# A Fourier stage on two column halves of the array, with one evacuation per PSUM bank, late inputs prepared later, and a load split over two queues

## The chip, the cores and the metric

The kernel runs on one core of a Trainium2 chip. The metric is the device time of one execution in microseconds (us). All runs told here are of the fast state (the granted TensorE clock is 0.97 of full speed on average in all of them). "TensorE" is called PE in the profile and its weight loads PEld; VectorE is DVE, ScalarE is ACT, GpSimd is POOL, SyncE is SP. PSUM is the memory that takes TensorE's results, in banks; an evacuation is the copy that moves a bank's content out of it. A unit is the work on four channels: two calls of the transform stage.

## The reference

A long convolution (by FFT along the sequence), then a maxout FFN:

```python
def _attn_ref(x, v, pos_emb, w1, w2):              # B=4, S=12544, D=128
    h_filt = (np.maximum(pos_emb @ w1, 0.0) @ w2) * window
    u = x * v
    L = 2 * S
    Uf = np.fft.rfft(u, n=L, axis=1)
    Hf = np.fft.rfft(h_filt, n=L, axis=0)
    y = np.fft.irfft(Uf * Hf[None, :, :], n=L, axis=1)[:, :S, :]
    return (x * y).astype(np.float32)

def _moe_ref(x, w1, w2, w3, w_out):                # 50176 tokens, 768 hidden
    h = np.maximum(np.maximum(x @ w1, x @ w2), x @ w3)
    return h @ w_out
```

Everything is float32. The kernel writes 12544 as 98 x 128. Its first transform stage is a 98-point transform over one index, as a matmul with the constant `f1` (98 x 196: 98 columns of real parts, 98 of imaginary parts).

## The kernel before

`first` is the stage that changes. One call handles two channels: two matmuls of 98 rows, 128 weight columns (`lhs[i]`: two interleaved halves r of 64 points) and 196 moving columns. The result lies in one PSUM bank with r on the partitions and (channel, real/imaginary c, frequency k) on the columns. `spec` wants c on the partitions, so four copies of 64 partitions move it, two on each engine.

```python
    def first(ps, lhs, at):
        for i in range(2):
            nc.tensor.matmul(ps[:, i * 2 * NB:(i + 1) * 2 * NB], lhs[i], f1[:],
                             start=(i == 0), stop=True, skip_group_check=True)
        for r in range(2):
            for c in range(2):
                src = ps[64 * r:64 * r + 64, 0:4 * NB].rearrange(
                    "p (s c k) -> p c k s", s=2, c=2)[:, c]
                dst = spec[64 * c:64 * c + 64, :, r, at:at + 2]
                if r == 0:
                    nc.scalar.copy(dst, src)
                else:
                    nc.vector.tensor_copy(dst, src)
```

It is called 64 times for the filter (stretch A), 64 times for batch 0 (32 units of two calls, stretch B), and 64 times for each of batches 1 to 3, there between the FFN's matmuls of the batch before:

```python
    def u_first(u):                      # one unit: two calls
        t = uts.pop(u)
        for i in range(2):
            ps = state["turn"][1].tile([P, 512], FP32, tag="cv", name="ps1")
            first(ps, [...], 4 * u + 2 * i)
    # ... stretch B (the first NPRE = 20 units are transposed beforehand)
    for u in range(NU):
        u_first(u)
        v = u + NPRE
        if v < NU:
            u_mul(v)                     # VectorE: x * v of a late unit
        if u and v - 1 < NU:
            u_turn(v - 1)                # TensorE: its four transpositions
            if v + 2 < NU:
                u_load(0, v + 2)
    # ... beside the FFN, one unit in 1.9 slots of the FFN
            at(s, u_turn, u)
            at(s + 1, u_first, u)
```

For each of 49 groups of frequencies, `g_load` brings weights and the filter's spectrum `ht` (two halves of 64 partitions) through SyncE's queue.

## Time and profile before

| stretch | us | what sets it |
|---|---|---|
| A: filter's first stage, 86.33 to 137.73 | 51.4 | VectorE's copies |
| A to B: second stage of the filter, preparations of batch 0 | 93.6 | loads |
| B: batch 0's first stage, 231.28 to 305.74 | 74.5 | late loads, then copies |
| batch 0's groups alone, to the first FFN work | 247.1 | serial work of VectorE and ScalarE |
| long part, from 552.82 | 2293.0 | TensorE |
| whole execution | 2847.86 (median) | |

A and B run to the first record of the second stage (L144); the long part starts at the first record of L477. A row of the windows has the length of the stretch, then each engine's busy time with the number of its records, the granted clock, the DMA engines' busy share and GB/s. A float32 matmul leaves two records.

### The profile page before, as it was taken

The numbers are of one execution on the slowest core, as the hardware profiler recorded it, in microseconds if no ns is written. First come the engines' busy times: TensorE is split into PE (matmuls) and PEld (weight loads), VectorE is DVE, ScalarE is ACT, GpSimd is POOL, SyncE is SP. The second block draws the span as 40 slices with busy tenths as digits, with TensorE's granted clock in tenths as the row PEclk, the third lists the DMA queues.
The fourth block names the chain that finished last, engine by engine and source line by source line (L and its number), as shares of the span: only waits on it lengthen the run. The fifth ranks groups of instructions, "written<-read, shape, count | busy, mean of one in ns | idle before, by whom it ended". The sixth has DMA issues, their size and how long they took to land.

```text
span 2845.9 us, 38675 instructions
## 1 busy us (share of the span) xinstructions
PE 2650.9 (93%) x13277; PEld 1926.9 (68%) x13277; DVE 1539.4 (54%) x3265; ACT 1196.9 (42%) x2571; POOL 26.9 (1%) x53
## 2 busy tenths in 40 slices
PE   6967665599999999999999999999999999999999
PEld 6866655477777676677777676777767766666665
DVE  3866777555466666355566665454666663222222
ACT  2635544344444444344444443444444442222222
POOL 0021000000000000000000000000000000000000
PEclk9988777799999999999999999999999999999999
DMA  3198599644577776444678774445687872222221
GB/s 78 38 354 230 156 266 280 193 105 100 139 212 220 212 220 185 110 98 108 173 215 222 221 217 129 105 113 142 183 224 216 223 197 68 57 57 57 56 56 34
DMA packets 455348, 446.12 MB, mean 157 GB/s; under 512 B 292746, under 2 KB 344432, under 8 KB 454960
## 3 DMA queue, kind: packets, MB, share of 16 engines
q1 hardware_dynamic: 329392, 353.27, 46.9%
q10 hardware_dynamic: 121840, 77.52, 9.3%
q0 software_dynamic: 3920, 12.85, 1.2%
q8 instruction: 106, 1.74, 0.3%
q14 instruction: 90, 0.74, 0.1%
HBM read 353.61 MB, written 89.92 MB: 156 GB/s over the span
## 4 chain that ended last, share of the span: by engine, by line
PE 75%; ACT 3%; DMA 2%; ACTq 0%; DVE 0%; issue 0%; SPq 0%; DVEq 0%
PE pa L489 17%; PE pb L492 17%; PE ops L500 17%; PE yps L477 8%; PE ps L128 4%; PE ps L420 4%; PE ps L144 3%; PE ops L499 3%; PE pst L356 1%; DMA ht<-hd 1%; ACT xs L395 1%; ACT xs L394 1%; ACT zs L424 1%; DMA zt<-zd 1%; ACT hid L490 1%; ACT eo L156 0%
## 5 line engine op out<-in xcount | busy, mean ns | idle before, releaser
L493 DVE TENSOR_TENSOR hid<-hid,pb 128x392 f32<-128x392 f32 x768 | 431.3, 562 | 582.4 <-PE pb L492 468.5
L489 PE MATMUL pa<-gt,w_sb 128*128 128x392 f32 x1536 | 638.2, 497 | 11.8 <-ACT hid L490 11.2
L490 ACT ACTIVATE hid<-pa 128x392 f32<-128x392 f32 x768 | 382.5, 498 | 615.1 <-PE pa L489 541.2
L492 PE MATMUL pb<-gt,w_sb 128*128 128x392 f32 x1536 | 632.0, 493 | 1.2 <-ACT hid L490 1.2
L500 PE MATMUL ops<-hid,wo_sb 128*128 128x392 f32 x1536 | 630.9, 492 | 0.1
L492 PEld LDWEIGHTS pb<-gt,w_sb 128*128 128x128 f32 x1536 | 289.8, 190 | 218.6 <-DVE hid L493 25.5
L500 PEld LDWEIGHTS ops<-hid,wo_sb 128*128 128x128 f32 x1536 | 291.7, 190 | 214.2 <-DVE hid L493 0.7
L489 PEld LDWEIGHTS pa<-gt,w_sb 128*128 128x128 f32 x1536 | 258.2, 191 | 114.5 <-ACT hid L490 45.3
L420 PE MATMUL ps<-ab,wt 128*128 128x128 f32 x1568 | 231.8, 295 | 96.1 <-DVE ab L411 96.1
L138 DVE COPY spec<-ps 64x196 f32<-64x196 f32 x640 | 235.6, 368 | 149.1 <-ACT spec L136 139.8
L420 PEld LDWEIGHTS ps<-ab,wt 128*128 128x128 f32 x1568 | 217.6, 205 | 139.6 <-issue 68.8
L144 PE MATMUL ps<-spec,wt 128*128 128x128 f32 x1960 | 287.8, 298 | 9.8 <-DVE spec L138 9.8
L144 PEld LDWEIGHTS ps<-spec,wt 128*128 128x128 f32 x1960 | 273.9, 215 | 24.6 <-issue 10.3
L136 ACT COPY spec<-ps 64x196 f32<-64x196 f32 x640 | 214.8, 336 | 166.0 <-PE ps L128 154.0
L477 PEld LDWEIGHTS yps<-f,zt 98*128 98x128 f32 x2048 | 250.5, 193 | 43.2 <-DMA zt<-zd 7.9
L400 DVE TENSOR_TENSOR xt<-xt,ht 128x512 f32<-128x512 f32 x196 | 135.5, 691 | 241.7 <-ACT xs L395 234.4
L477 PE MATMUL yps<-f,zt 98*128 98x98 f32 x2048 | 248.1, 274 | 7.6 <-DMA zt<-zd 7.6
L424 ACT COPY zs<-ps 128x512 f32<-128x512 f32 x196 | 114.9, 586 | 259.0 <-PE ps L420 246.2
L394 ACT ACTIVATE xs<-xt 64x512 f32<-64x512 f32 x196 | 123.0, 628 | 171.3 <-DVE xt L151 138.5
L128 PEld LDWEIGHTS ps<-f,uT 98*128 98x128 f32 x1024 | 175.9, 193 | 25.1
L481 DVE TENSOR_TENSOR gt<-yps,xT 128x392 f32<-128x392 f32 x128 | 72.5, 566 | 221.7 <-PE yps L477 210.6
L128 PE MATMUL ps<-f,uT 98*128 98x196 f32 x1024 | 192.4, 334 | 0.0
(58 smaller groups left out, 1710.2 us busy)
## 6 DMA issues: line engine op xcount, KB each, us to landing
wt<-wt_const SPq DMA_DIRECT2D x220, 512.0 KB
ht<-hd SPq DMA_DIRECT2D x392, 256.0 KB
zd<-zs ACTq DMA_DIRECT2D x196, 256.0 KB
zt<-zd SPq DMA_DIRECT2D x128, 392.0 KB
ut<-in_xr_dram SPq DMA_DIRECT2D x128, 196.0 KB
ut<-in_vr_dram SPq DMA_DIRECT2D x128, 196.0 KB
xT<-in_x_dram SPq DMA_DIRECT2D x512, 49.0 KB
out_dram<-ot ACTq DMA_DIRECT2D x128, 196.0 KB
```

The lines of the kernel that those rows point to most:

```text
L128: nc.tensor.matmul(ps[:, i * 2 * NB:(i + 1) * 2 * NB], lhs[i], f1[:], start=(i == 0), stop=True, skip_group_check=True)
L136: nc.scalar.copy(dst, src)
L138: nc.vector.tensor_copy(dst, src)
L144: nc.tensor.matmul(ps[:, (2 * k + r) * D:(2 * k + r + 1) * D], w[:, k, r, :], spec[:, 2 * g + k, r, :], start=(k == 0 and r == 0), stop=Tr ...
L394: nc.scalar.mul(xs[0:64], xt[64:128], -1.0)
L420: nc.tensor.matmul(ps[:, (2 * k + q) * D:(2 * k + q + 1) * D], w[:, 1, k, q, :], ab[:, k, q, :], start=(k == 0 and q == 0), stop=True, ski ...
L477: nc.tensor.matmul(ps[:, s * NB:(s + 1) * NB], zt[:, c, s * D:(s + 1) * D], f4[:, c, :], start=(s == 0 and c == 0), stop=(c == 1), skip_gr ...
L489: nc.tensor.matmul(pa[:, 0:N], w_sb[1][:, f * P:(f + 1) * P], rhs, start=True, stop=True)
L490: nc.scalar.activation(h[:], pa[:, 0:N], Relu)
L492: nc.tensor.matmul(pb[:, 0:N], w_sb[2][:, f * P:(f + 1) * P], rhs, start=True, stop=True)
L493: nc.vector.tensor_tensor(out=h[:], in0=h[:], in1=pb[:, 0:N], op=ALU.max)
L500: nc.tensor.matmul(pos_[i][:, 0:N], wo_sb[:, f, :], h[:], start=False, stop=(f == NF - 1))
```

## The change

The intent is to turn four 64-partition copies into one 128-partition copy. TensorE computes real and imaginary parts into different partitions: the array is used as two halves of 64 columns, c = 0 and c = 1, each with the same weights and its own half of `f1`. The bank then has c on the partitions, as `spec` has. Besides, the late units of B are multiplied and transposed six units later, and one half of `ht` goes to GpSimd's queue.

```diff
-    def first(ps, lhs, at):
+    def first(ps, lhs, at, copy):
         for i in range(2):
-            nc.tensor.matmul(ps[:, i * 2 * NB:(i + 1) * 2 * NB], lhs[i], f1[:], ...)
-        for r in range(2):
-            for c in range(2):
-                ... four copies, r == 0 on ScalarE, r == 1 on VectorE
+            for r in range(2):
+                for c in range(2):
+                    nc.tensor.matmul(
+                        ps[64 * c:64 * c + 64, (2 * i + r) * NB:(2 * i + r + 1) * NB],
+                        lhs[i][:, 64 * r:64 * r + 64], f1[:, c * NB:(c + 1) * NB],
+                        start=(i == 0 and r == 0), stop=True, skip_group_check=True)
+        copy(spec[:, :, :, at:at + 2],
+             ps[:, 0:4 * NB].rearrange("p (s r k) -> p k r s", s=2, r=2))
+    copies = (nc.scalar.copy, nc.vector.tensor_copy)     # calls take them in turn
@@ g_load
-        for half in range(2):
-            nc.sync.dma_start(
+        for half, eng in enumerate((nc.sync, nc.gpsimd)):
+            eng.dma_start(
@@ stretch B
-        v = u + NPRE
-        if v < NU:
+        v = u + NPRE - 6
+        if NPRE <= v < NU:
             u_mul(v)
-        if u and v - 1 < NU:
+        if NPRE <= v - 1 < NU:
             u_turn(v - 1)
```

More of the change, by code (lines that the diff above doesn't have):

```diff
@@ L123, in load_w2 @@
         return w
-    def first(ps, lhs, at):
+    def first(ps, lhs, at, copy):
         for i in range(2):
-            nc.tensor.matmul(ps[:, i * 2 * NB:(i + 1) * 2 * NB], lhs[i], f1[:],
-                             start=(i == 0), stop=True, skip_group_check=True)
-        for r in range(2):
-            for c in range(2):
-                src = ps[64 * r:64 * r + 64, 0:4 * NB].rearrange(
-                    "p (s c k) -> p c k s", s=2, c=2)[:, c]
-                dst = spec[64 * c:64 * c + 64, :, r, at:at + 2]
-                if r == 0:
-                    nc.scalar.copy(dst, src)
-                else:
-                    nc.vector.tensor_copy(dst, src)
+            for r in range(2):
[7 more added lines that the diff above has]
+    copies = (nc.scalar.copy, nc.vector.tensor_copy)
     def second(ps, w, g):
@@ L319 @@
         ps = fps.tile([P, 512], FP32, tag="ps", name="ps3")
-        first(ps, [hs[:, d + i].rearrange("n r t -> n (r t)") for i in range(2)], d)
+        first(ps, [hs[:, d + i].rearrange("n r t -> n (r t)") for i in range(2)], d,
+              copies[d // 2 % 2])
     filt.close()
@@ L365, in u_first @@
             first(ps, [t[:, 2 * i + j].rearrange("n r t -> n (r t)") for j in range(2)],
-                  4 * u + 2 * i)
+                  4 * u + 2 * i, copies[i])
     def g_load(g):
```

## The prediction

> **What bounds the kernel now.** I first read the windows (busy time of each engine by stretch), because the page shows that the run has stages with different limits. The change touches two short stretches and every batch after them: A, the filter's transform (86.33 to 137.73 us); B, batch 0's transform (231.28 to 305.74 us); then batch 0's groups alone; then the long part from 543 us, in which the transform of the next batch runs beside the FFN.
>
> ```profile
> core 0: us, PE busy (x) PEld busy (x) DVE busy (x) ACT busy (x) POOL busy (x), PEclk, DMA share, GB/s
> 86.33:137.73 51.40, 46.12 (x256) 41.39 (x257) 46.82 (x128) 41.20 (x128) 0.00 (x0) 0.99 0.06 16
> 231.28:305.74 74.46, 55.26 (x307) 50.54 (x305) 56.27 (x148) 49.16 (x142) 2.70 (x5) 0.88 0.50 133
> 305.74:543.00 237.26, 141.40 (x776) 131.19 (x776) 166.58 (x343) 107.35 (x195) 0.00 (x0) 0.75 0.92 253
> 569.50:764.00 194.50, 194.50 (x897) 140.93 (x896) 100.03 (x225) 95.48 (x228) 0.00 (x0) 1.00 0.49 118
> ```
>
> See that TensorE is never idle in the last row, a transform stretch beside the FFN; there are three, one for each later batch. VectorE and ScalarE are half idle there, so work taken off them is worth nothing. In A, VectorE is the busiest; in B nobody is full.
>
> The chain of waits within the third of these stretches says what TensorE pays for one unit there (two calls of the transform, eight matmul records), and what stands on either side:
>
> ```profile
> 572.63 0.66 PE ops L500 x2
> 573.29 1.33 PE ps L128 x8
> 574.62 0.66 PE pa L489 x2
> ...
> 588.69 1.76 PE yps L477 x16
> 590.45 0.44 PE pst L356 x4
> ```
>
> So a record of 196 columns costs 1.33/8 = 0.166 us of TensorE time and a call 0.665 us. The 98-column records with 128-column weights (L477) cost 1.76/16 = 0.110 us, although half of 0.166 is 0.083: there the weight load sets the pace.
>
> Third, the groups, for what the evacuations cost now and what one large evacuation costs:
>
> ```profile
> L138 DVE COPY spec<-ps 64x196 f32<-64x196 f32 x640 | 235.6, 368 | 149.1 <-ACT spec L136 139.8
> L136 ACT COPY spec<-ps 64x196 f32<-64x196 f32 x640 | 214.8, 336 | 166.0 <-PE ps L128 154.0
> L506 ACT COPY ot<-ops 128x392 f32<-128x392 f32 x128 | 62.3, 487 | 89.2 <-PE ops L500 89.2
> L481 DVE TENSOR_TENSOR gt<-yps,xT 128x392 f32<-128x392 f32 x128 | 72.5, 566 | 221.7 <-PE yps L477 210.6
> ```
>
> VectorE waits for ScalarE on every tile, then copies twice: 2 x 0.368 = 0.74 us a call against TensorE's 0.665. Last, the waits in A and in B:
>
> ```profile
> PE ps L144 <- DVE spec L138: 5.3, 1, 5.3
> ...
> PE pst L356 <- DVE ut L349: 14.5, 5, 7.5
> PE ps L144 <- DVE spec L138: 4.5, 1, 4.5
> ```
>
> The 5.3 us end A: TensorE has finished and waits for VectorE's backlog of copies. The other two are B's: 14.5 us in which a transposition of unit 20 or later stands in TensorE's order before transforms whose inputs are ready, and its data are still coming from memory; and 4.5 us of backlog at the end.
>
> **What the Trainium skill says.** "TensorEngine Tiling (Array Packing)", section Tiling Modes: an array of 128x64 is two tiles that load and multiply in parallel, but changing the tiling mode, not just the tile, drains the engine. "TensorE: Matmul & The Clock Gate", section Part 3: three column tiles gave 2.38 times the throughput at 512 columns. The trace before has no two column tiles on the same rows; it has 64x64 tiles on different rows (L265 and L280), whose records do interleave, 0.02 us apart. It also shows a drain:
>
> ```profile
> 23.91 0.83 PE L265 MATMUL ps<-spec,w_sb 64*64 64x34 f32 x7
> 24.06 0.54 PEld L265 LDWEIGHTS ps<-spec,w_sb 64*64 64x64 f32 x4
> 24.67 0.18 PEld L250 LDWEIGHTS pw<-eye,win 98*128 98x128 f32 x1
> ...
> 25.77 0.75 PE L253 MATMUL pw<-back,winT 128*98 128x128 f32 x2 [0.67 <-ACT winT L251]
> 26.44 0.39 PEld L265 LDWEIGHTS ps<-spec,w_sb 64*64 64x64 f32 x3 [0.27 <-issue]
> ```
>
> Normally a weight load begins while the matmul before it streams. Here, on both changes of mode and with no semaphore to wait for, it begins only about when the matmuls before it end (23.91 + 0.83 = 24.74; 25.77 + 0.75 = 26.52). "DMA: Bandwidth & Descriptors", section Issuing engines are not separate DMA queues: a second issuing engine saves only the issue time. The trace before cannot show that for these loads, all of which SyncE issues.
>
> **The change part by part.**
>
> *Matmuls.* A call goes from 2 matmuls (4 records of 196 columns) to 8 (16 records of 98 columns, 64-column weights), in pairs on the two column halves. If the pairs overlap fully, it costs 8 x 0.083 = 0.66 us, plus some 2 ns a record: 0.68 us, the same as now. It has half the array twice as often.
>
> *Mode changes.* In the long part each unit stands between full-array matmuls, so two changes of mode a unit. My estimate: a drain of about 0.12 us after the last column has streamed (24.67 less 24.45, where the last record starts, less 0.107 for its streaming), twice, plus the weight load that is no longer hidden: 0.105 us for 128 columns (half of it for 64). L128's first record after idleness lasts 433 ns against 329 of the later ones, which is that 0.104. Together 2 x 0.12 + 0.105 + 0.053 = 0.40 us a unit. There are 3 x 32 = 96 units on the bound engine: +38 us; with 96 x 2 calls x 0.015 us of record overhead, +41 us.
>
> *Copies.* Four of 64x196 become one of 128x392, in turn on ScalarE (about 0.49 us by L506) and VectorE (about 0.57 by L481), each with its bank to itself. A pair of calls then takes 0.57 us of the slower engine instead of 1.47, so TensorE becomes the bound of A: 64 x 0.68 = 43.5, plus matmul latency and a last copy, 44.5 us instead of 51.4; TensorE also no longer idles for 5 us and so needn't restart on a slow clock (48 records after that wait took 8.55 us, 0.178 each, against 0.110), some 2 us more. A: -9 us.
>
> *B.* The order lets six units of transforms run before the first multiplication of late inputs, so most of the 14.5 us is filled with work: about -9. The backlog of 4.5 us at the end goes, and VectorE's pace in the last 25 us (62 copies in 24.01 us, 0.387 each, so 1.55 us a unit against TensorE's 1.33 to 1.40) doesn't bind: about -6 with the clock. Against it 12 transpositions with two changes each, 12 x 0.40 = 5, of which some fall in waits: +2. B: -13 us.
>
> *Spectrum's halves.* 196 of 392 loads of 256 KB go to GpSimd's queue. In the stretch alone no wait for them appears; its period of 4.8 us is VectorE's and ScalarE's serial work, so 0. Beside the FFN TensorE waits 7.6 us for one load and that one is a store's round trip. At most a few us: -2.
>
> Sum of the main case: 2848 + 41 - 9 - 13 - 2 = 2865 us.
>
> **The rivals.**
>
> *No drain that matters*, because a column split with all rows may not be a change of the same kind as 128 to 64x64, the only one seen. Then +3 instead of +41 and B is -15: 2848 + 3 - 9 - 15 - 2 = 2825. For it: the whole change would be pointless to a tuner otherwise. Against: the gap stands in the trace for both directions.
>
> *Weight loads become the pace.* Two 64-column loads of 0.053 us each for a pair of records, if the two halves cannot load at once from the same rows, give 0.107 a pair and 0.86 a call. L477 shows such pacing. Then 96 x 2 x 0.19 = +36 on top; A grows to 56 us and B hardly gains: about 2930 with the drain, 2885 without.
>
> *The halves run one after the other*: 16 x 0.083 = 1.33 us a call, +0.66 x 192 = +127 in the long part and +35 in A, +20 in B: over 3020 even before drains. For it: both halves stream different columns from the same partitions, which no record before shows. Against: the skill's measured 2.38.
>
> *GpSimd's loads come late* in the stretch alone, where the DMA share is 0.92 already. With four buffers a load has about three periods, 14 us; half of a microsecond more of issue does no harm. I give it little.
>
> **Range and chances.** I weigh full overlap with the drain at 0.42, full overlap with little drain at 0.28, weight-paced at 0.17, serial at 0.08, the rest unforeseen. The middle lies between the first two, so I say 2852 us. The 8-in-10 range reaches from a little under the no-drain case to the weight-paced case, 2812 to 2925. Faster by over 2% means under 2791, which needs a gain in the long part that I see no source for: 0.05. Slower by over 2% means over 2905: most of the weight-paced case with drain, the serial case, and a drain twice as long as estimated: 0.22. Within 2%: 0.73.
>
> **What would show it.** Right: in the changed profile a unit's transform has records of c = 0 and c = 1 starting 0.02 us apart, at 0.085 us a pair; the weight load on either side of a unit starts only as the matmul before it ends; a transform stretch of the long part grows from 194.5 us by some 13; A is near 42 us, B near 61, TensorE waits under 1 us for the copies at the end of each; the stretch alone stays at 237. Wrong: pairs at 0.107 or records one after the other, weight loads that run ahead across the mode change, or a transform stretch of the long part that gets shorter.

## The result, and the profile after

The changed kernel takes 2861.43 us (median of 4 runs, 2859.91 to 2863.67); the kernel before took 2848.52 in the same rounds. The ratio is 1.0046, 95% interval 1.0028 to 1.0063. A ratio is the mean time of one kernel's fast runs over that of the other's of the same rounds, so it is not quite the ratio of the medians quoted. The change was forecast at 2852, with a main case of 2865. Measured, it is slower by 0.5%, which the interval sets clear of zero.

The windows of the changed kernel, for the same stretches as in the prediction (A, B, the groups alone, the first transform stretch beside the FFN):

```profile
85.88:129.91 44.03, 43.31 (x1024) 43.15 (x1025) 18.15 (x32) 16.23 (x32) 0.00 (x0) 1.00 0.01 3
223.67:286.58 62.91, 55.13 (x1073) 50.06 (x1073) 26.70 (x52) 23.74 (x46) 4.53 (x8) 0.95 0.61 157
286.58:524.00 237.42, 139.57 (x776) 129.45 (x776) 166.34 (x341) 107.28 (x195) 28.49 (x49) 0.77 0.97 255
551.08:755.31 204.23, 204.23 (x1661) 139.82 (x1660) 70.16 (x129) 67.53 (x131) 0.00 (x0) 1.00 0.46 110
```

A shrank from 51.4 to 44.0 us, B from 74.5 to 62.9. In A, VectorE's 46.82 us of work became 18.15, and TensorE is busy throughout. The transform stretch beside the FFN grew from 193.2 to 204.2 us (first to last record of the stage), although VectorE and ScalarE do some 30% less there: TensorE was the bound and still is. Between the two profiles the spans differ by 16.0 us: A -7.4, B -11.6, the long part +34.8, the rest +0.2.

The chain of waits (start, length, engine, line, number of records) says where TensorE's extra time goes:

```profile
571.69 1.76 PE yps L478 x16
573.45 0.44 PE pst L357 x4
...
595.88 0.66 PE ops L501 x2
596.54 1.50 PE ps L131 x32
598.04 0.85 PE pa L490 x2
```

The neighbours that keep the whole array cost what they did, 1.76, 0.44 and 0.66. A unit's transform costs 1.50 instead of 1.33, and whatever stands behind it 0.19 more: 0.85 instead of 0.66. That is 0.36 us a unit, 96 times, 34.6 us.

The timeline of the same place, with the weight loads:

```profile
595.72 0.82 PE L501 MATMUL ops<-hid,wo_sb 128*128 128x392 f32 x2
...
596.47 1.38 PEld L131 LDWEIGHTS ps<-f,uT 98*64 98x64 f32 x32 [0.56 <-issue]
596.47 1.57 PE L131 MATMUL ps<-f,uT 98*64 98x98 f32 x32
...
597.97 0.30 PEld L490 LDWEIGHTS pa<-gt,w_sb 128*128 128x128 f32 x2
597.97 0.60 PE L490 MATMUL pa<-gt,w_sb 128*128 128x392 f32 x1
```

Here is the mechanism. Thirty-two records of 98 columns fit into 1.57 us because c = 0 and c = 1 run together: in the single records (which the timeline merges), the two of a pair start 0.006 to 0.008 us apart, and pairs follow each other every 0.0842 us. A call costs 8 x 0.0842 = 0.674 us, against 0.665 before. But the first weight load of the unit begins at 596.470, and the last record of L501 begins at 596.049 and streams for 0.329 us, to 596.378. So TensorE waits 0.092 us until it may load, and 0.053 more for the first 64 columns (the second pair starts at 596.607, less 0.084): 0.145 us to get in. On the way out the last pair has streamed at 597.869, the load of L490 begins at 597.967, and its first matmul streams from 598.075 (its second starts at 598.402, less 0.327): 0.206 us. The `[0.56 <-issue]` says that the loads waited for nothing that the profile shows, no semaphore. The other units show the same: over all 96 of the long part the two pauses before a load are 0.091 to 0.094 and 0.097 to 0.098 us. The trace shows the pause and not its reason; "drain" is the prediction's name for it. Below, a mode change is the switch between the whole array and its halves, and a stretch of split work lies between two such changes.

The groups (busy time and mean ns of one, then idle time before it and its releaser) show the evacuations:

```profile
L135 DVE COPY spec<-ps 128x392 f32<-128x392 f32 x160 | 90.5, 567 | 198.4 <-PE ps L131 198.4
L135 ACT COPY spec<-ps 128x392 f32<-128x392 f32 x160 | 80.8, 505 | 215.5 <-PE ps L131 215.5
```

Two calls cost VectorE 0.567 us instead of 4 x 0.368 = 1.47, and ScalarE 0.505 instead of 1.34. Both now wait for TensorE only.

TensorE's waits within B of the changed kernel:

```profile
PE pst L357 <- DVE ut L350: 4.0, 1, 4.0
PE ps L131 <- issue: 2.4, 2, 1.4
PE ps L144 <- issue: 0.7, 1, 0.7
PE ps L131 <- DVE xs L151: 0.6, 2, 0.4
```

The wait for late inputs fell from 14.5 to 4.0 us, and that for VectorE's backlog at the end, 4.5 us before, is gone: 0.7 remains.

### The profile page after: what moved, and what is told of

It reads as the page before. It is cut to its first block, busy times and chain, and to the rows that moved or that the text cites. A ratio compares the mean times of both kernels' runs of the same rounds, so it can differ in the third digit from the quotient of the medians.

```text
span 2861.9 us, 45221 instructions
## 1 busy us (share of the span) xinstructions
PE 2678.7 (94%) x17117; PEld 1923.2 (67%) x17117; DVE 1392.8 (49%) x2785; ACT 1063.7 (37%) x2091; POOL 142.1 (5%) x249
## 4 chain that ended last, share of the span: by engine, by line
PE 74%; ACT 3%; DMA 3%; ACTq 1%; issue 0%; SPq 0%; DVE 0%; DVEq 0%
PE pa L490 17%; PE pb L493 16%; PE ops L501 16%; PE yps L478 7%; PE ps L131 5%; PE ps L421 4%; PE ps L144 3%; PE ops L500 3%; DMA zd<-zs 2%; PE pst L357 2%; DMA wt<-wt_const 1%; ACT zs L425 1%; ACT xs L396 1%; ACT xs L395 1%; ACT hid L491 1%; ACTq L426 0%
## 5 line engine op out<-in xcount | busy, mean ns | idle before, releaser
L490 PE MATMUL pa<-gt,w_sb 128*128 128x392 f32 x1536 | 647.5, 503 | 11.8 <-ACT hid L491 11.1
L501 PE MATMUL ops<-hid,wo_sb 128*128 128x392 f32 x1536 | 630.9, 492 | 0.1
L501 PEld LDWEIGHTS ops<-hid,wo_sb 128*128 128x128 f32 x1536 | 291.8, 190 | 214.1 <-DVE hid L494 0.7
L490 PEld LDWEIGHTS pa<-gt,w_sb 128*128 128x128 f32 x1536 | 252.9, 191 | 125.3 <-ACT hid L491 45.9
L375 POOL DMA_DIRECT2D ht<-hd x196 | 115.2, 588 | 1995.7 <-DVE xs L405 1912.9
L131 PEld LDWEIGHTS ps<-f,uT 98*64 98x64 f32 x4096 | 177.2, 137 | 54.5 <-issue 52.6
L131 PE MATMUL ps<-f,uT 98*64 98x98 f32 x4096 | 199.1, 251 | 3.0 <-issue 2.4
L135 DVE COPY spec<-ps 128x392 f32<-128x392 f32 x160 | 90.5, 567 | 198.4 <-PE ps L131 198.4
```

Source lines behind the costliest of these rows:

```text
L131: nc.tensor.matmul(ps[64 * c:64 * c + 64, (2 * i + r) * NB:(2 * i + r + 1) * NB], lhs[i][:, 64 * r:64 * r + 64], f1[:, c * NB:(c + 1) * NB ...
L490: nc.tensor.matmul(pa[:, 0:N], w_sb[1][:, f * P:(f + 1) * P], rhs, start=True, stop=True)
L501: nc.tensor.matmul(pos_[i][:, 0:N], wo_sb[:, f, :], h[:], start=False, stop=(f == NF - 1))
```

## The experiments

Each was timed against the kernel before on the same chip. "Changed" is the kernel above; the edits are to it unless said otherwise. All nine runs gave correct results. The stretches are from one profile each; profiles with the same code in B and the same work around it differ there by up to 0.9 us (62.6 to 63.5 in the changed kernel and experiments 1 to 3).

### 1. Full array again beside the FFN

```diff
-            at(s + 1, u_first, u)
+            at(s + 1, u_first, u, True)     # True: the old first() with its four copies,
+                                            # for batches 1 to 3 only
```

> Only the transforms beside the FFN go back to full-array matmuls with four copies; A, B and the queues stay as changed. Theory (mode changes cost the long part): its three batches return to their old length, minus 34 us from 2861, so about 2828, ratio to before 0.993, and a transform stretch of the long part is 193 us again (from first to last transform record) instead of 204. Rival (GpSimd's half of the spectrum loads slows the long part): the stretch stays near 204 and the time near 2860. Rival (more records and weight loads cost TensorE time): same total as the theory, so this run cannot tell that one; the runs with calls apart and units paired do.

Measured: 2828.95 us, ratio 0.9927 (0.9914 to 0.9939). The transform stretch is 193.2 us again, the long part 2294.1; A (44.0) and B (62.6) keep their gains. A unit's transform and what stands behind it cost what they did before the change:

```profile
560.87 1.33 PE ps L140 x8
562.20 0.66 PE pa L507 x2
```

So the whole loss lies in this use of the split array, and GpSimd's loads, still there, do not slow the long part. This version is 0.7% faster than the kernel before: the interval is clear of 1.

### 2. The two calls of a unit apart

```diff
-            at(s + 1, u_first, u)
+            at(s + 1, u_first, u, (0,))
+            at(s + 2, u_first, u, (1,))
```

> The same matmuls, but the two calls of a unit stand in different slots beside the FFN, so the order has 194 stretches of split-array work instead of 110, 84 more pairs of mode changes. Theory: 84 x 0.35 = +29 us over the changed kernel, about 2891, ratio to before about 1.015. Rival (cost goes with the number of records): nothing, 2861. Rival (a change of mode costs only the weight load, 0.16 us a pair): +13, 2874.

Measured: 2885.55 us, ratio 1.0127 (1.0113 to 1.0141). The chain shows each call paying the toll by itself:

```profile
575.20 0.82 PE ps L131 x16
576.02 0.85 PE pa L491 x2
```

Two calls now cost 2 x 0.82 and two neighbours 0.85. (Of the 192 calls beside the FFN, 24 still stand two together, so there are 180 stretches there.) The count of records is the same as in the changed kernel, so the rival that charges for records falls. The 25.9 us that the long part grew over the changed kernel's (2353.7 less 2327.8) is 0.31 us for each of 84 more stretches, nearer to the full change of mode (0.35) than to the weight load alone (0.16). The total is some 5 us under the theory's 2891 and 12 over the 2874 of that rival.

### 3. Two units together

```diff
-            at(s + 1, u_first, u)
+            if u % 2:
+                at(s + 1, u_first, u - 1)
+                at(s + 1, u_first, u)
```

> The same matmuls, but beside the FFN two units' transforms stand together: 62 stretches of split-array work instead of 110, 48 fewer. Theory: 48 x 0.35 = -17 us, about 2844.5, ratio to before about 0.9986. Rival (cost goes with records): 2861. If four PSUM tiles in a row make TensorE wait for evacuation, the gain is smaller and waits of L131 for ScalarE or VectorE appear.

Measured: 2846.53 us, ratio 0.9986 (0.9971 to 1.0002).

```profile
594.67 2.85 PE ps L131 x64
597.52 0.85 PE pa L492 x2
```

Two units cost 2.85 instead of 2 x 1.50, and only one neighbour pays. No wait of L131 for an evacuation appears in the long part. With the kernel before (no split stretches there), this one (48), the changed kernel (96) and the one with calls apart (180), the long part takes 2293.0, 2311.8, 2327.8 and 2353.7 us. The three split ones lie on a line: 0.317 us a stretch ((2353.7 - 2311.8)/132) and 3.6 us once, and for 96 stretches this gives 2327.0. Of the 3.6 us the slower pitch of the pairs makes up 192 x 0.009 = 1.7; the rest was not traced, but the long part of five profiles with full-array transforms there ranges from 2293.0 to 2295.6 us by itself.

### 4. One queue for the spectrum

```diff
-        for half, eng in enumerate((nc.sync, nc.gpsimd)):
+        for half, eng in enumerate((nc.sync, nc.sync)):
```

> The changed kernel with both halves of the spectrum issued by SyncE again. Theory (the queue is worth nearly nothing): 2861 within 5 us; the stretch of batch 0's groups alone stays at 247 us. Rival (the second queue is what makes B or the long part shorter): B from 62.9 us to 66 or more, or the group stretches of the long part grow, 5 to 15 us in all. Rival (GpSimd's loads harm): 3 to 8 us faster.

Measured: 2863.72 us, ratio 1.0051 (1.0038 to 1.0065), which overlaps the changed kernel's interval. B is 64.5 us instead of 62.9, a batch of the long part 621.0 instead of 620.4; the groups alone take 246.5 against 247.5. The second queue is worth 2 us or so at best, and in the total it is not clear of noise.

### 5. The old order in B

```diff
-        v = u + NPRE - 6
-        if NPRE <= v < NU:
+        v = u + NPRE
+        if v < NU:
@@
-        if NPRE <= v - 1 < NU:
+        if u and v - 1 < NU:
```

> The changed kernel with the late multiplications and transpositions of batch 0 back at the start of stretch B. Theory (about 9 of B's 11.5 us come from filling the wait for late inputs): B goes from 62.9 to about 71 us, total about 2869. Rival (B's gain is the copies', the order is worth nothing): B stays near 63, total 2861.

Measured: 2870.6 us, ratio 1.0076 (1.0061 to 1.0091). B is 71.5 us. TensorE's long waits in B are back:

```profile
PE pst L357 <- DVE ut L350: 12.9, 2, 8.0
```

Taken out of the changed kernel, the order is worth 8.6 us of B's 11.6.

### 6. The kernel before with the new order alone

```diff
 # to the kernel before
-        v = u + NPRE
-        if v < NU:
+        v = u + NPRE - 6
+        if NPRE <= v < NU:
@@
-        if u and v - 1 < NU:
+        if NPRE <= v - 1 < NU:
```

> The kernel before with the new order of stretch B alone. Theory (order and copies each give part of B): B goes from 74.5 to about 68, the backlog of VectorE's copies at its end stays near 4.5 us, A and the long part as before: about 2842. Rival (order alone gives all of B): B about 63, total 2837. Rival (order worth nothing without the shorter copies, since VectorE then sets B's pace): B 73 or more, 2847.

Measured: 2840.37 us, ratio 0.9970 (0.9956 to 0.9985). B is 66.8 us, 7.7 less; A is unchanged at 51.4. In B:

```profile
PE ps L144 <- DVE spec L138: 4.4, 1, 4.4
PE pst L356 <- DVE ut L349: 3.6, 6, 2.0
```

The wait for inputs has gone from 14.5 to 3.6 us, the backlog at the end stays. Order and copies are two parts of B's gain: 7.7 to 8.6 us for the order and 3.0 to 3.9 for the copies, depending on which is taken first. This edit alone, without the split array, is already 8 us better than the kernel before.

### 7. One half after the other

```diff
-        for i in range(2):
-            for r in range(2):
-                for c in range(2):
+        for c in range(2):
+            for i in range(2):
+                for r in range(2):
```

> The changed kernel with the four matmuls of the left column half before the four of the right, instead of in turn. Theory (TensorE overlaps neighbours on different tiles and looks only a few records ahead, as the 64x64 tiles of the kernel before did, where the second tile's first record came after the fifth of eight): a call costs 0.85 to 1.0 us instead of 0.67; 0.25 x 320 calls, A grows to some 58 us, a transform stretch of the long part by 16, total about 2920. Rival (the look-ahead covers eight records): 2861. Rival (no overlap at all): 1.35 a call, total above 3050.

Measured: 2925.14 us, ratio 1.0270 (1.0253 to 1.0287). A takes 51.5 us. In A a call takes 0.787 us instead of 0.674, and a unit beside the FFN takes 2.00 us of the chain instead of 1.50:

```profile
589.18 2.00 PE ps L131 x32
591.18 0.86 PE pa L490 x2
```

The predicted 0.85 to 1.0 us a call was too high for A, where calls follow each other and one call's right half overlaps the next one's left. The expected total of 2920 came out close, but not term by term: its 0.25 us on 320 calls would alone be 80 us. A grew by 7.5 us instead of some 14; B, which the text leaves out, by 4.5 (67.4 us); a transform stretch beside the FFN, where a unit stands alone, by the expected 16 (204.2 to 220.2).

With eight records of one half in a row, the halves overlap only in part. In the records of A, the first record of a half starts 0.006 us after the fifth of the other half's eight and before its sixth. So three records of the half that comes first in the program start after the first of the other half: the start order is not strictly the program's. The second of the 64x64 tiles of the kernel before started at the same place (at 63.359 us, after the first tile's fifth record at 63.353).

### 8. Full array beside the FFN, and late transpositions in threes

```diff
 # to the kernel of experiment 1, in stretch B: after units 9, 13, 17, 21 multiply three late
 # units, after units 10, 14, 18, 22 transpose them and load the next three
+        k, step = divmod(u - 9, 4)
+        late3 = range(NPRE + 3 * k, NPRE + 3 * k + 3) if 0 <= k < 4 else ()
+        if step == 0: ...  u_mul(w)
+        if step == 1: ...  u_turn(w); u_load(0, w + 3)
```

> A candidate that beats both: as with full-array transforms beside the FFN, and in B the twelve late transpositions in four groups of three, so eight fewer pairs of mode changes there and later needs for late loads. Theory: 8 x 0.35 = 3 us, and 2 to 4 us of waiting for inputs: B about 57 us, total about 2822, ratio to before 0.991. If it falls, the loads of three units at once arrive late and transpositions wait for them.

Measured: 2824.55 us, ratio 0.9916 (0.9901 to 0.9931). B:

```profile
223.28:280.81 57.53, 52.74 (x1074) 49.87 (x1073) 26.35 (x52) 23.24 (x46) 4.53 (x8) 0.97 0.62 174
```

B is 5.4 us shorter than in the changed kernel; TensorE's busy time in it fell by 2.4 us, about the 2.8 of eight pairs of mode changes. By the ratios the total lies 3 us lower than in experiment 1, but their intervals overlap, so the gain over that one is shown in B, not in the total.

### 9. The kernel before, one engine per bank

```diff
 # to the kernel before: all four copies of a bank on one engine, banks in turn
-                if r == 0:
-                    nc.scalar.copy(dst, src)
-                else:
-                    nc.vector.tensor_copy(dst, src)
+                copy(dst, src)
```

> The kernel before with its full-array matmuls and four 64-partition copies a call, but all four of a bank on one engine, ScalarE and VectorE taking banks in turn. Theory (A was paced by the number of VectorE's copies, two a call on average before and here too): A stays about 51 us, within 1; the total about 2848. Rival (the hand-over of a bank from ScalarE to VectorE was the cost, so one engine per bank is what helps): A about 45, B shorter by 4, total about 2838.

Measured: 2845.43 us, ratio 0.9989 (0.9972 to 1.0006). A is 50.2 us, 1.2 less than before, a shade outside the 1 us that the theory allowed and far from the rival's 45. At the end of A:

```profile
PE ps L143 <- DVE spec L135: 5.2, 1, 5.2
```

The backlog is still there. What helps is fewer and larger copies: VectorE's busy time in A is 46.1 us here, 46.8 before and 18.2 in the changed kernel. The hand-over from ScalarE to VectorE within a bank can have cost no more than the 1.2 us.

## Why the prediction was right

**What bounds what.** Right: VectorE set A, TensorE the long part. Taking 30 us of VectorE's and 28 us of ScalarE's work out of one transform stretch beside the FFN gave nothing there (experiment 1 puts that work back, with the full array, and the stretch is as long as before the change).

**Matmuls overlap.** Right: 0.674 us a call, 0.68 predicted. The prediction gave the weight-paced and serial rivals a quarter together; pairs every 0.0842 us exclude both. Experiment 7 shows what the order of the matmuls adds: the overlap has to be arranged. More records cost 0.009 us a call (0.674 less 0.665), not 0.015.

**Mode changes.** Right in kind, a fifth too high in size: 0.40 us a unit was predicted, 0.351 read off a unit's records, 0.317 a stretch from the line of experiments 2 and 3. The term that was too large is the drain: 0.12 us each way was estimated at the start of the run, and 0.092 and 0.098 were measured in the long part; the two weight loads came out as estimated, 0.161 us together against 0.158. TensorE is slower at that early place (the four weight loads of L265 before the gap take 223 ns each, against a median of 135); that this is the reason was not tested. The long part grew by 34.8 us instead of 41.

**A.** The term for the copies was right: 44.0 us against 44.5. The 2 us for not restarting on a slow clock failed, and the sign "A is near 42" counted them within A, though they fall after it. The clock part itself happened (the granted clock of the first 4.27 us was 0.50 before, and 1.00 in the first 5.59 us after), as the first records of the second stage show, before and after:

```profile
137.73 8.55 PE L144 MATMUL ps<-spec,wt 128*128 128x128 f32 x48 [5.28 <-DVE spec L138]
```

```profile
129.91 5.60 PE L144 MATMUL ps<-spec,wt 128*128 128x128 f32 x48 [0.71 <-issue]
```

But the 2.95 us saved did not reach the end: the stretch from A to B is paced by loads (DMA share 1.03 before, 1.07 after), TensorE waits there for late units, and these are its waits before and after:

```profile
PE pst L356 <- DVE ut L349: 26.3, 16, 3.6
```

```profile
PE pst L357 <- DVE ut L350: 29.0, 17, 4.7
```

It does the work sooner and waits 2.7 us longer; the stretch is 93.8 us against 93.6. This stretch varies more than the 2.95 us from profile to profile, 92.3 to 95.5, but its mean is 93.7 over the eight profiles with split matmuls in A and 93.9 over the three without: no gain there.

**B.** Predicted -13, measured -11.6: 7.7 to 8.6 by the order (9 predicted, experiments 5 and 6) and the other 3.0 to 3.9 by the copies with the split array. That part was put at 6, less 2 for mode changes, so it was put a little high. (One reading was off without effect: VectorE's last 62 copies take 23.9 us in the trace, not 24.01. B came to 62.9 us, against the sign "near 61".)

**The queues.** Predicted -2, measured within noise of that (experiment 4).

**The number.** The stated 2852 is a hedge between the case with the drain (2865) and the case without (2825), and no mechanism gives it. Measured was 2861, because the drain was there. That the main case came so near is partly luck: against the difference of the two profiles (16.0 us, 17 in the main case) the long part's loss was put 6 us too high, and the savings of A, B and the queues 5 us too high as well. The reading of the trace before, two weight loads that did not run ahead, carried this; it deserved more weight than the thought that a tuner would not have made the change for nothing. Why the change was made stays open; experiment 1 shows that the part in A and B is good.

## What to carry to other kernels

In this kernel, splitting the array paid where evacuation was the bound and many split matmuls stood together; where TensorE was the bound and split work alternated with full-array work, each stretch of split work cost about 0.3 us, so batch it or keep the full array there. Order matmuls of different tiles in turn, not one tile after the other. Before counting a gain on an engine, ask which engine ends each stretch: the same edit gained 7 us in one stretch and lost 35 in another.

## What the Trainium skill lacked or had wrong

- "TensorEngine Tiling (Array Packing)", section Tiling Modes, says that a change of mode drains TensorE, without a size. Here: 0.145 us from the whole array to two 64-column halves and 0.206 us back, of which 0.092 and 0.098 us pass before the next weight load may begin and the rest is that load, no longer hidden.
- "TensorE: Matmul & The Clock Gate", section Part 3, says in its list of what overlaps that a weight load overlaps matmuls in flight only when the row group differs (the paragraph above that list also allows a load into the background weight buffer). Here both halves use the same 98 rows, and their 32 loads of 137 ns in a unit (4.4 us in all) lie within 1.38 us, beside the matmuls.
- The same section doesn't say how far apart two tiles' matmuls may stand in the order and still overlap. Here: in turn, two records at a time, 0.674 us a call; eight records of one half, then eight of the other, 0.787 us in a run of calls and 2.00 us of the chain against 1.50 for a unit that stands alone.
